# Second token parity wholly in Strassen groups, with the first parity's WO rows in place of its plain slots

## The chip, the cores and the metric

The kernel runs on one core of a Trainium2 chip. The metric is the device time of one execution in microseconds (us), as the median of several runs. A profiled execution gives the trace; its span goes from the first to the last instruction.

## The reference

For 2048 tokens of width D = 576 in float32 the reference normalises x and adds an attention and a feed-forward network that read the same normalised rows:

```python
x = A_x
xn = _layernorm(x, axis=-1)
return x + _A_ref(xn, A_wqkv, A_wo) + _B_ref(xn, B_w1, B_w2)
```

`_A_ref` projects xn by wqkv to q, k, v of 32 heads of 18, lets each token attend to 8 tokens (itself and the ones 2, 4, ... 14 before it), and multiplies the result by wo. `_B_ref` is `relu(xn @ w1) @ w2` with 4608 hidden columns. Since all distances in the attention are even, tokens of even and of odd position never meet.

## The kernel before

**Two parities.** The 1024 even tokens (ph 0) are worked off first, then the 1024 odd ones (ph 1). Each parity has four token blocks (tb) of 256 tokens. Every float32 operand is cut into a rounded high part and the remainder (`two`, L171: ACT writes the high part, VectorE or GpSimd the low one), and each product is made of three matmul terms: high x high, high x low, low x high. A matmul covers 64 of the 128 rows of the array; two of them, on the lower and the upper 64 rows, run at a time (`mm_rows`, `rows`), so work is counted in pairs. D is 4 x 128 + 64; the last 64 rows are the remainder.

**Plain slots.** A slot n is one block of 128 hidden columns f for one token block. For two slots `h_two` makes h with 14 + 13 pairs of 256 columns, `h_out` applies relu and cuts the result, and `o_two` makes the output matmuls of one slot, 6 pairs of 256 and 6 of 320 columns. The slots of a parity are numbered from `BASE[ph]`; each parity does its first 6 of 36 hidden blocks in 24 plain slots (`NOLD`). Lists by slot (`at`, `first`, `late`) place the other work between them: loads, cuts, the projection of the first head unit, the T sums, the preparation of the first Strassen pair.

**Strassen groups.** The remaining hidden blocks are taken two by two (a pair p). For a pair and 512 tokens a group g makes the 2 x 2 x 2 product of (2 x 128 hidden) x (2 x 256 of D) x (2 x 256 tokens) with 7 products in place of 8 (`PROD`, `M`), each 6 pairs, and adds the 64-row remainder (`R`, 6 pairs). It needs sums of W1's quarters, S1 to S4 (`sw_load`, `sw_mix`, `sw_prep`, staged in `ST`, put at the places in `MAT`), and sums of x^T's quarters, T1 to T4 (`ts_steps`, run in portions by `ts_run`). T1 to T4 of 512 tokens serve all groups of a parity. A group has eight steps; each step is 6 pairs of product and 6 pairs of output matmuls of the group before (`o_half`). Other work hangs on steps by `on(ph, g, i, "T" or "O", ...)`, and `ins` puts projections there. `prologue` is group 0, with the last plain output matmuls as filler; `tail_end` finishes a parity's last group. Before the change there are 15 pairs and 30 groups in each parity.

**Attention.** Heads are worked in four units u of 8 heads (`QKV_G` says with which group a unit's projection begins; unit 0 is projected among plain slots, at `UNIT0`). Its VectorE work waits in a queue, from which `run_bg` takes what fits. The result goes to DRAM (`od`), comes back transposed in four rows r of 256 tokens (`ot_in`, L697: one load of 512 KB and two of 64 KB), is cut by ACT and VectorE in two halves (`ot_split`, L708), and multiplied by wo (`wo_half`, four quarters a row, 54 pairs). `ot_plan` lists these steps with their conditions; `ot_go(ph)` does the next one that is due, `ot_go(ph, r)` does all that row r needs now. `evict` (L746) copies finished output tiles from PSUM on ACT and adds them to the output in DRAM with an accumulating DMA from GpSimd's queue; those of WO rows wait until the adds of all four token blocks have landed (`ADDED`).

**Between the parities.** x^T of the second parity is made early: normalised, turned, written to DRAM, and loaded back by `xt_in` (one load of 512 KB, two of 64 KB) into the buffer that the first parity's block leaves; `xt_parts` cuts it. In `seam` the first parity's last group ends with plain h matmuls of the second parity as filler, then WO row 0 follows; rows 1, 2 and 3 of the first parity stand at the second parity's slots 3 and 6. SyncE's queue (SP) issues all loads in the order of the program, each when its destination is free.

## Time and profile before

| | us |
|---|---|
| median of 3 runs (lowest, highest) | 1102.11 (1101.01, 1102.72) |
| profiled execution | 1100.51 |
| its span | 1098.7 |
| TensorE matmul busy | 1091.6 (99%) |
| VectorE busy | 837.8 (76%) |
| ScalarE busy | 573.3 (52%) |
| GpSimd busy | 269.7 (25%) |

PE is TensorE, PEld its weight loads, DVE VectorE, ACT ScalarE, POOL GpSimd, SP SyncE, and a q behind a name is that engine's queue. A row of a group of instructions names line, engine, operation, output<-input with their shapes and the count; behind the bar stand the busy time in us, the mean duration of one in ns, and the idle time of the engine before them with what ended it. A row of waits names who waited for whom, us in all, how often and the longest. In a timeline the first two numbers are start and length. A row of DMA issues gives the count, the KB of each, and the us from issue to landing. L numbers are lines of the kernel before.

### The profile page before, as it was taken

Reading aid. Unit: us, or ns where it says so; the run is one execution under the profiler, and the core shown is the slowest. Engines: PE = TensorE matmul, PEld = TensorE weight load, DVE = VectorE, ACT = ScalarE, POOL = GpSimd, SP = SyncE. Lnnn points to the kernel's source line nnn. Section 1 sums busy time; section 2 is a strip of 40 time slices with the busy share of each in tenths; the row PEclk is TensorE's granted clock in tenths of the full one; section 3 lists DMA queues with packets and bytes.
Section 4 is the critical chain, followed back from the end, with each engine's and each line's share of the span. In section 5 each row is a group of like instructions: output and inputs, shape, how many; then the busy total and the mean of one; then the engine's idle time right before and its main releaser. Section 6 shows DMA issues by size and latency. Waiting matters only on the chain.

```text
span 1098.7 us, 37877 instructions
## 1 busy us (share of the span) xinstructions
PE 1091.6 (99%) x16410; PEld 1085.1 (99%) x16410; DVE 837.8 (76%) x1379; ACT 573.3 (52%) x1353; POOL 269.7 (25%) x260
## 2 busy tenths in 40 slices
PE   9999999999999999999999999999999999999998
PEld 8999999999999999999999999999999999999998
DVE  7676888897997988994424549987989978998741
ACT  5433564564465356656634345635635644666551
POOL 2311421222222122322211022212212222223221
PEclk9999999999999999999999999999999999999999
DMA  7469995696598498889968159849947965988896
GB/s 227 149 158 225 176 200 98 146 214 116 104 231 145 72 224 160 156 151 255 271 94 188 24 119 188 149 77 198 183 88 162 207 113 109 220 148 168 163 226 150
DMA packets 136599, 177.26 MB, mean 161 GB/s; under 512 B 27873, under 2 KB 83937, under 8 KB 136401
## 3 DMA queue, kind: packets, MB, share of 16 engines
q0 software_dynamic: 37632, 81.40, 46.8%
q1 hardware_dynamic: 98080, 92.55, 29.4%
q8 instruction: 129, 2.11, 0.8%
q10 hardware_dynamic: 720, 0.89, 0.2%
q14 instruction: 38, 0.30, 0.1%
HBM read 74.07 MB, written 96.22 MB: 155 GB/s over the span
## 4 chain that ended last, share of the span: by engine, by line
PE 98%; DVE 1%; DMA 0%; ACT 0%; issue 0%; DVEq 0%; POOL 0%; ACTq 0%
PE po L163 34%; PE po L142 22%; PE ph L163 16%; PE pm L163 12%; PE pm L142 5%; PE ph L142 4%; PE ph L130 1%; PE po L130 1%; PE pm L354 0%; DMA att<-in_x 0%; DVE pr L575 0%; DMA words<-att 0%; PE pm L130 0%; DVE ar L176 0%; DVE att L419 0%
## 5 line engine op out<-in xcount | busy, mean ns | idle before, releaser
L163 PE MATMUL po<-ar 64*128 64x320 f32 (+1 forms) x5688 | 474.2, 289 | 0.1
L163 PEld LDWEIGHTS po<-ar 64*128 64x128 f32 x5688 | 416.3, 184 | 0.8 <-PE ph L163 0.4
L163 PE MATMUL ph<-xT,ar 64*128 64x256 f32 x2520 | 319.1, 274 | 1.0 <-DVE ar L807 1.0
L163 PEld LDWEIGHTS ph<-xT,ar 64*128 64x128 f32 x2520 | 287.7, 184 | 1.3 <-DVE ar L807 1.2
L762 POOL DMA_DIRECT2D out<-ev x126 | 151.4, 1201 | 554.4 <-ACT ev L756 391.1
L163 PE MATMUL pm<-xS,ar 64*128 64x256 f32 x2160 | 259.6, 274 | 0.0
L163 PEld LDWEIGHTS pm<-xS,ar 64*128 64x128 f32 x2160 | 238.4, 184 | 0.2
L756 ACT ACTIVATE ev<-po 128x640 f32<-128x640 f32 (+1 forms) x260 | 168.4, 652 | 132.7 <-PE po L163 75.3
L176 DVE TENSOR_TENSOR ar<-st,ar 128x256 fp32r<-128x256 f32 (+3 forms) x236 | 126.4, 556 | 58.7 <-ACT ar L172 56.5
L172 ACT ACTIVATE ar<-st 128x256 fp32r<-128x256 f32 (+3 forms) x304 | 146.6, 504 | 3.8 <-DMA st<-in_w 2.2
L142 PE MATMUL po<-wq,xT 64*128 64x432 f32 x1296 | 136.9, 354 | 0.0
L142 PEld LDWEIGHTS po<-wq,xT 64*128 64x128 f32 x1296 | 123.5, 184 | 1.9
L174 POOL TENSOR_TENSOR ar<-st,ar 128x256 fp32r<-128x256 f32 (+1 forms) x68 | 76.2, 1122 | 134.9 <-ACT ar L172 96.4
L163 PE MATMUL ph<-xS,ar 64*128 64x256 f32 x720 | 101.6, 274 | 0.0
L163 PEld LDWEIGHTS ph<-xS,ar 64*128 64x128 f32 x720 | 94.2, 184 | 0.1
L610 DVE TENSOR_TENSOR pr<-att 128x1152 f32<-128x1152 f32 x64 | 87.9, 1386 | 0.4
L575 DVE TENSOR_TENSOR pr<-att 128x1152 f32<-128x1152 f32 x64 | 86.3, 1359 | 0.1
L578 DVE TENSOR_REDUCE att<-pr 128x64 f32<-128x1152 f32 x64 | 85.8, 1345 | 0.0
L142 PE MATMUL po<-ar 64*128 64x256 f32 (+1 forms) x984 | 74.2, 289 | 0.0
L617 DVE TENSOR_TENSOR pr<-pr 128x1152 f32<-128x1152 f32 x64 | 68.9, 1076 | 1.4
L807 DVE SCALAR_TENSOR_TENSOR ar<-ph,ar 128x256 fp32r<-128x256 f32 x99 | 40.4, 420 | 37.7 <-ACT ar L803 37.5
L142 PEld LDWEIGHTS po<-ar 64*128 64x128 f32 x984 | 67.8, 184 | 0.3
(127 smaller groups left out, 1365.9 us busy)
## 6 DMA issues: line engine op xcount, KB each, us to landing
out<-ev POOLq DMA_DIRECT2D x126, 576.0 KB, 7.2
st<-in_w SPq DMA_DIRECT2D x72, 288.0 KB, 5.1
st<-in_w SPq DMA_DIRECT2D x63, 256.0 KB, 3.4
att<-att SPq DMA_DIRECT2D x16, 441.0 KB, 4.5
att<-in_wqkv SPq DMA_DIRECT2D x28, 216.0 KB, 6.2
od<-att SPq DMA_DIRECT2D x32, 160.0 KB, 6.1
att<-in_x SPq DMA_DIRECT2D x14, 288.0 KB, 4.0
st<-in_w SPq DMA_DIRECT2D x60, 64.0 KB, 6.1
```

Source lines behind the costliest of these rows:

```text
L142: ins = nc.tensor.matmul(o, l[z], r[z], start=start, stop=stop)
L163: b.ins = nc.tensor.matmul(b.ap, l[part], r[part], start=start, stop=stop, skip_group_check=skip)
L172: nc.scalar.activation(hi, src, AF.Copy)
L174: nc.gpsimd.tensor_tensor(lo, src, f32(hi), op=ALU.subtract)
L176: nc.vector.tensor_tensor(lo, src, f32(hi), op=ALU.subtract)
L575: nc.vector.tensor_tensor(pr[i], q, window(k, i), op=ALU.mult)
L578: nc.vector.tensor_reduce(lg[:, i], pr.pop(i).rearrange(heads, d=Dh), axis=AX.X, op=ALU.add)
L610: nc.vector.tensor_tensor(pr[i].rearrange(heads, d=Dh), e, window(v, i).rearrange(heads, d=Dh), op=ALU.mult)
L617: nc.vector.tensor_tensor(o, z[:, :, 0:n], z[:, :, n : 2 * n], op=ALU.add)
L756: nc.scalar.activation(acc[:, :, cols], z[:, :, 0 : cols.stop - cols.start], AF.Copy)
L762: ADDED[ph, tb] = nc.gpsimd.dma_start(rows_of(ph, tb), acc, accum_op=ALU.add)
L807: nc.vector.scalar_tensor_tensor(lo, src, 0.0, f32(hi), op0=ALU.max, op1=ALU.subtract)
```

## The change

The first parity stays as it was. The second parity has no plain slots any more: all its 36 hidden blocks are 18 pairs, 36 groups.

- `NP`, `NG` and the first hidden block `F0` now depend on the parity; `MAT` is one layout for both; a group number below 0 of the second parity means a group at the end of the first.
- The seam ends the first parity as the epilogue ends the second (`tail_pieces`), with output matmuls alone as filler. Then WO rows 0 and 1 follow back to back. The new `prologue` takes a function for its filler: for the second parity these are the quarters of WO rows 2 and 3, the last two of them in group 1.
- The T sums are made from the loaded x^T before it is cut (`apart`: four differences in place of four additions and four differences). Their steps and the cuts of x^T stand in a queue `side`, of which three are done after each quarter of a WO row.
- W1's first pair of the second parity is loaded, mixed and prepared in the last two groups of the first, two of its preparations in the seam.
- The projection of unit 0 moves into groups 3 and 4; units 1 to 3 come at groups 9, 15 and 21.
- The loads of WO rows 0 and 1 are allowed earlier (steps 4 and 5 of the last group), row 2's when the tail is done, row 3's when row 0 is done, into row 0's place.
- The room for two of the last evictions of the first parity is in pool xS in place of pr. The fourth mix of the first parity's pair 1 goes to GpSimd like its other three.

```diff
-UNIT0 = (10, 12)
-QKV_G = {0: -2, 1: 5, 2: 11, 3: 17}
+UNIT0 = 10
+QKV_G = ({1: 5, 2: 11, 3: 17}, {0: 3, 1: 9, 2: 15, 3: 21})
...
+    F0 = (NC0 * C, 0)
+    NP = [(NF - f) // 2 for f in F0]
+    NG = [2 * n for n in NP]
...
+        def apart(m, xt, k, b):
+            half = lambda z: z.rearrange("p (k c) -> p k c", k=2)
+            less_of = half(raw(b)) if isinstance(b, int) else f32(b[0][:, b[1] : b[1] + 2, :])
+            nc.vector.tensor_tensor(half(raw(m)), f32(xt[:, k : k + 2, :]), less_of, op=ALU.subtract)
+            dve(512)
+
+        if ph:
+            return [
+                (apart, 0, t2, 0, (t1, 0)), (apart, 1, t2, 2, (t2, 0)), (apart, 2, t2, 2, 0), (apart, 3, t1, 2, 2),
+                (cut, 0), (cut, 1), (cut, 2), (cut, 3),
+            ]
...
-        if r < 3:
-            z = ot_arena(ph)[:, r * OTW : (r + 1) * OTW]
+        if r < 3 or ph == 0:
+            k = r % 3
+            z = ot_arena(ph)[:, k * OTW : (k + 1) * OTW]
...
+        if g < 0:
+            ph, g = ph - 1, g + NG[ph - 1]
...
-        on(ph, NG - 1, 5, "O", hold.__setitem__, ("xs", ph), True)
-        on(ph, NG - 1, 1, "O", last_room, ph)
-        if ph == 0:
-            for i in range(2):
-                on(ph, NG - 1, 4 + i, "O", xt_in, 1, i)
-            on(ph, NG - 2, 4, "O", w1_load, 1, 0)
-            on(ph, NG - 1, 5, "O", w2_load, 1, 0)
-            on(ph, NG - 1, 5, "O", hold.__setitem__, ("go", 0), True)
-            on(ph, NG - 1, 5, "O", ot_go, 0)
...
+            on(ph, g, 4, "O", last_room, ph)
+            on(ph, g, 4, "O", xt_in, 1, 0)
+            on(ph, g, 4, "O", hold.__setitem__, ("go", 0), True)
+            on(ph, g, 4, "O", ot_go, 0)
+            on(ph, g, 5, "O", xt_in, 1, 1)
+            on(ph, g, 5, "O", hold.__setitem__, ("go", 1), True)
+            for i in (6, 7, 8):
+                on(ph, g, i, "O", ot_go, 0)
...
+    def sums(tp):
+        side.extend([(ts_run, 1, tp, 1)] * 4)
+        for i in range(4 * tp, 4 * tp + 4):
+            side.extend([(xt_parts, 1, i, 0), (xt_parts, 1, i, 1)])
+        side.extend([(low_twin, 1, 2 * tp)] + [(ts_run, 1, tp, 1)] * 4)
...
+        def more(k):
+            ot_go(0)
+            if k > 1:
+                xt_in(1, k)
+
+        tail_pieces(0, more, lambda: ot_go(0))
+        hold["go", 2] = True
+        for i in range(2):
+            w2_load(1, i)
+        sums(0)
+        side.extend([(sw_prep, 1, 0, "S3", "S4"), (sw_prep, 1, 0, "A22", "rem")])
+        for r in range(2):
+            for k in range(4):
+                ot_go(0, r) if k == 0 else ot_go(0)
+                wo_half(0, r, k % 2, k > 1)
+                aside(3)
+                if k == 2:
+                    ot_go(0, r + 1)
+            if r == 0:
+                hold["go", 3] = True
+        sums(1)
+
+    def wo_fill(n):
+        if n >= 8:
+            aside(len(side))
+            return
+        r, k = 2 + n // 4, n % 4
+        if k == 0:
+            ot_go(0, r)
+        wo_half(0, r, k % 2, k > 1)
+        ot_go(0)
+        aside(3)
+        if n == 1:
+            ot_go(0, 3)
...
+    prologue(0, old_fill)
+    for g in range(1, NG[0]):
+        group(0, g)
+    seam()
+    prologue(1, wo_fill)
+    for g in range(1, NG[1]):
+        group(1, g)
+    epilogue()
```

## The prediction

> **What bounds the kernel now.** I read the page first, then the waits of TensorE, then the stretch where the first parity ends (the seam): its engines by window, its chain, and the DMA queues.

> ```profile
> span 1098.7 us, 37877 instructions
> PE 1091.6 (99%) x16410; PEld 1085.1 (99%) x16410; DVE 837.8 (76%) x1379; ACT 573.3 (52%) x1353; POOL 269.7 (25%) x260
> ```
> ```profile
> PE po L119 <- POOL mhalf L114: 1.4, 1, 1.4
> PE ph L163 <- DVE ar L807: 1.0, 1, 1.0
> PE ph L130 <- ACT xT L359: 0.7, 1, 0.7
> PE pm L354 <- ACT att L338: 0.5, 1, 0.5
> ```
> TensorE waits 3.6 us in all, so the time is its list of matmuls, and a matmul less is time less as long as nothing new runs late. The prices, from the chain (half of a plain pair of slots, 28 matmuls; one whole WO row, 108), from the timeline (last two: 12 matmuls each) and from the windows (length, then busy time of PE, PEld, DVE, ACT, POOL, then the granted clock, DMA share, GB/s):

> ```profile
> 537.26 1.60 PE ph L142 x28
> 547.29 7.08 PE po L142 x108
> ```
> ```profile
> 1044.11 0.84 PE L163 MATMUL ph<-xT,ar 64*128 64x256 f32 x12
> 1044.79 0.84 PE L163 MATMUL po<-ar 64*128 64x256 f32 x12
> ```
> ```profile
> 515.57:530.01 14.44, 14.44 (x208) 13.77 (x209) 10.47 (x23) 11.95 (x29) 3.74 (x4) 1.00 1.10 277
> 1041.19:1052.87 11.68, 11.68 (x197) 11.68 (x194) 5.20 (x10) 7.76 (x20) 4.05 (x4) 1.00 1.03 255
> 1055.79:1066.45 10.66, 10.66 (x157) 10.31 (x154) 5.58 (x12) 6.87 (x14) 3.27 (x3) 1.00 1.04 207
> 1095.20:1098.70 3.50, 0.00 (x0) 0.00 (x0) 0.76 (x2) 0.00 (x0) 0.00 (x0) 0.90 0.46 156
> ```
> The 64-row matmuls run two at a time, so I count pairs. A plain pair of 256 columns costs 1.60/14 = 0.114 us, one in a Strassen group (1044.79 - 1044.11)/6 = 0.113 us. A whole group takes 11.68 us.

> **Term 1: the matmuls.** 24 plain slots of the second parity leave, 13.5 pairs each for h, 324 in all. In their place stand 6 groups: 7 products of 6 pairs and 6 pairs of remainder are 48, so 288. The output matmuls (12 pairs for a slot, 48 for a group), the four WO rows and the projections are as many as before. 36 pairs x 0.114 = **4.1 us less**; 72 matmuls fewer, 16338 on the page.

> **Term 2: the end of the first parity.** The seam took 14.44 us until its first WO row, with 27 pairs of plain h in it (27 x 0.114 = 3.08): 11.36 for the rest. The same tail at the end of the kernel, with only output matmuls as filler, took 10.66. The new seam has that second form and ACT no longer cuts x^T in it: **0.7 less**. Bounds: nothing, if ACT is as late as before, to 1.1, if no wait is left.

> **Term 3: the WO rows, now back to back.** Before, row 0 began at 530.01 and row 1 at 547.29, and rows 2 and 3 came after that. Now row 0 follows the tail (515.57 + 10.66 = 526.23), row 1 follows at 533.3, the first products at 540.39, and row 2 at 540.39 + 0.68 = 541.07. The row needs its 640 KB of attention output loaded and cut in two halves by ACT (L713) and DVE (L714). What speaks against that is DMA:

> ```profile
> DMA  9999999999999999999999999999999999999999
> q0 software_dynamic: 478, 1.06, 56.4%
> q1 hardware_dynamic: 1607, 1.69, 53.8%
> ```
> ```profile
> 516.20 1.59 SPq L706 DMA_DIRECT2D att<-od  x2
> 525.43 1.18 SPq L706 DMA_DIRECT2D att<-od  x2
> 534.66 1.64 SPq L706 DMA_DIRECT2D att<-od  x2
> ```
> ```profile
> att<-od SPq DMA_DIRECT2D x2, 64.0 KB, 9.0
> ```
> ```profile
> att<-od SPq DMA_DIRECT2D x2, 64.0 KB, 10.5
> ```
> ```profile
> att<-od SPq DMA_DIRECT2D x2, 64.0 KB, 8.6
> ```
> ```profile
> SPq L706 <- DMA xT<-words: 6.0, 3, 2.9
> ```
> From 525 to 535 us all 16 DMA engines are busy, and SP's queue (q1) moves 1.69 MB in 10 us, 0.169 MB/us; SP issues a load only when an older one has landed (the last row). The small parts of the loads of rows 0, 1, 2 were issued at 516.20, 525.43 and 534.66 and landed 9.0, 10.5 and 8.6 us later (the three rows, in that order; the issue of the second part adds up to 1.6). So row 2's data was whole at 543.3 to 544.9, say 544.1, while it was needed only after row 1, at 547.29 + 7.08 = 554.4.

> In the changed kernel row 2's load is again behind four x^T loads and two row loads, but two transfers are gone ahead of it: W1's first chunk (768 + 2x96 KB) becomes one pair's load (2x256 + 2x64 KB), 320 KB less, and of three loads of W2 (288 KB) two are left.

> ```profile
> st<-in_w SPq DMA_DIRECT2D x1, 768.0 KB, 10.1
> st<-in_w SPq DMA_DIRECT2D x2, 96.0 KB, 9.7
> ```
> ```profile
> st<-in_w SPq DMA_DIRECT2D x72, 288.0 KB, 5.1
> st<-in_w SPq DMA_DIRECT2D x63, 256.0 KB, 3.4
> st<-in_w SPq DMA_DIRECT2D x60, 64.0 KB, 6.1
> ```
> That is 608 KB or 0.62 MB, 3.7 us at SP's rate: row 2 whole at 540.4. The work of ACT and DVE on it:

> ```profile
> L713 ACT ACTIVATE att<-att 128x640 fp32r<-128x640 f32 x12 | 8.6, 735 | 0.9 <-DMA att<-od 0.9
> L432 ACT ACTIVATE xT<-xT 128x512 fp32r<-128x512 f32 x8 | 4.9, 623 | 0.0
> L438 ACT ACTIVATE xT<-xT 64x128 fp32r<-64x128 f32 x8 | 2.5, 311 | 0.2
> L756 ACT ACTIVATE ev<-po 128x640 f32<-128x640 f32 x131 | 92.5, 706 | 80.6 <-PE po L163 74.4 <-PE po L142 6.0
> L714 DVE TENSOR_TENSOR att<-att 128x512 fp32r<-128x512 f32 x12 | 8.3, 692 | 8.6 <-ACT att L713 8.3
> ```
> Two halves are 1.47 us on ACT, and DVE's low part comes 0.69 after the second, when TensorE has four pairs (0.45) of its own to do: 540.4 + 1.47 + 0.69 - 0.45 = 542.1. TensorE waits **1.0 us**. Bounds: nothing (whole by 539.4), and 4.7, if the place in the queue decides and not the bytes (544.1). I take the bytes, since the engines' line is full. Behind the waiting ACT stand row 1's second eviction, then the seed of product bank q and the copy of m5; TensorE reaches their buffers 2 us after row 2 begins, so the wait is paid once. Row 3's load waits on SP for row 0's end, and behind it stand only loads of the next pair.

> **Term 4: what ACT has left.** Beside rows 0 and 1 (14.16 us) ACT now does: four x^T parts (0.623 + 2 x 0.311 each, 4.98), four T cuts and two preparations of 512 columns (6 x 0.623, 3.74), a twin (64 rows by 256, between those two prices: 0.4), four evictions (2.82), and the four halves of rows 1 and 2 (2.94): 14.9 us by durations. Activations overlap; in

> ```profile
> 537.91 0.73 ACT L713 ACTIVATE att<-att 128x640 fp32r<-128x640 f32 x1
> 538.54 0.62 ACT L432 ACTIVATE xT<-xT 128x512 fp32r<-128x512 f32 x1
> ```
> the second starts 0.63 after a first of 0.73, which makes it 12.9 us. 1.3 us are to spare. Late seeds here, and the first projection weights of the parity (loaded half a group, 5.8 us, ahead of their cut, where

> ```profile
> att<-in_wqkv SPq DMA_DIRECT2D x28, 216.0 KB, 6.2
> ```
> says 6.2) I put at **0.5 us**, between 0 and 1.5.

> ```profile
> L973 DVE TENSOR_TENSOR st<-st 128x256 f32<-128x256 f32 x117 | 60.2, 516 | 5.0 <-DMA st<-in_w 3.6 <-POOL st L973 1.2
> L176 DVE TENSOR_TENSOR ar<-st,ar 128x512 fp32r<-128x512 f32 x92 | 60.9, 686 | 11.3 <-ACT ar L172 11.0
> L176 DVE TENSOR_TENSOR ar<-st,ar 128x256 fp32r<-128x256 f32 x96 | 39.4, 429 | 9.3 <-ACT ar L172 9.0
> ```
> At nothing I cost: DVE's T sums (8 operations of 512 columns fewer, 0.69 each as in L714, beside WO rows that need DVE for little else), the mixes and preparations of three more pairs (4 x 0.516 + 3 x 0.686 + 2 x 0.429 = 5.0 us of DVE for each; the 11.68 us group above holds 5.20 of DVE with its share of this and no wait of TensorE; uncovered, 5.0 us in two groups would show as waits at products), the fourth mix of one pair from DVE to POOL, and the room for two evictions in xS in place of pr (free three steps later).

> Sum: -4.1 - 0.7 + 1.0 + 0.5 = **-3.3 us**. The profiled execution took 1100.51 us (its span and 1.8 around it), so 1097.2 for it; it lies 1.6 under the median of the three runs, 1102.11, and from that I predict **1098.8**. A measurement of this kernel can tell about 0.2%, 2.2 us, from no change.

> **Rivals.** *Row 2 stays late* (chance 0.22): DMA is as full as before, and the two adds of row 0 to the output, which run once the last add has landed, now come into the time of row 2's load. For it: both queues hold over half of the engines. Against: 608 KB fewer. By the old landing: -4.8 + 4.7 + 0.5 = +0.4, 1102.5, no change.

> *The clock falls in that wait* (0.07). After the last matmul the row of 1095.20 shows a mean clock of 0.90 over 3.5 us: if that is half speed, it began 2.8 us after the last matmul. A wait of 2.8 to 4.7 at row 2 would then run the next 2.3 us (a row's quarter and six pairs) at half speed: -4.8 + 3.5 + 2.3 + 0.5 = +1.5, 1103.6. [...]

> *ACT stands before row 1* (0.13, the slower side). Row 1's first half is cut on ACT during row 0, ahead of evictions and x^T parts. If its data is late, ACT holds everything: row 2 can start at landing + 12.9 + 0.24. Row 1's load is now the fourth, with the bytes that row 0's had ahead of it before plus 32 KB: 516.20 + 9.0 + 1.0 + 0.2 = 526.4, free up to 527.9. But if it slips behind the third x^T load as before, it lands at 525.43 + 10.5 = 535.9: row 2 at 549.0, 8.0 us late, -4.8 + 8.0 + 0.5 = +3.7, 1105.8. It decides from a landing at 534.4 on. Against it: in the program its order to load comes two steps before that x^T load.

> **How the numbers follow.** My forecast has 0.58, and it holds while the waits come to less than 2.6 us of the 4.8 gained. So faster 0.58, same 0.22 + 0.07 = 0.29, slower 0.13. The forecast alone spans 1097.3 (no wait) to 1099.9; the range goes from 1096.8, with the scatter of the runs, up over the two middle cases to 1103.6.

> **What would show it.** 16338 matmuls or close to it; the tail in about 10.7 us; a wait of TensorE for ACT or DVE (L713, L714) at the third WO row, of about 1 us; groups of 11.68 us in the second parity from its first on; the granted clock at 1.00. I am wrong if TensorE's new waits add up to over 2.6 us, if they stand at a product (T sums or S matrices late) and not at a WO row, or if groups 3 to 9 of the second parity, with their projections, take more than 11.68 us and what their projections cost before.

## The result and the profile after

The changed kernel takes 1108.02 us (median of 6 runs, 1107.0 to 1109.93) where the kernel before takes 1102.05 in the same series (6 runs, 1101.01 to 1102.72): a ratio of 1.0057, 95% interval 1.0044 to 1.007. It is slower by 0.6%, clear of the scatter; 1098.8 was predicted. The profiled execution took 1107.0 us, 6.5 more than the one before. The mean granted clock was 0.995 or 0.997 in all six executions (0.997 in the profiled one), so the half clock shown below is not of this execution alone.

Lines of the changed kernel have other numbers: matmuls of Strassen groups and output L160 (before L163), of WO rows L139 (L142), cuts of attention rows L722 and L723 (L713, L714), the mixes L977 (L973). L1045 is the copy that seeds a product bank, L1054 an addition to a kept product. From the page of the changed kernel:

```profile
span 1105.2 us, 37855 instructions
PE 1092.0 (99%) x16338; PEld 1081.9 (98%) x16338; DVE 844.1 (76%) x1402; ACT 590.8 (53%) x1396; POOL 274.1 (25%) x267
```
The waits of TensorE in the changed kernel:
```profile
PE ph L160 <- ACT ph L1045: 6.1, 2, 4.8
...
PE po L139 <- DVE att L723: 0.6, 2, 0.4
PE po L139 <- ACT att L722: 0.5, 2, 0.3
```
The matmuls are 16338, as counted, and yet PE is as long busy as before. The first row is new: two waits at a product, one of 4.8 us. In windows of the changed kernel (length, busy time of PE, PEld, DVE, ACT, POOL, granted clock, DMA share, GB/s) stand the end of the first parity, rows 0 and 1, row 2's first quarter with the six pairs ahead of it, the last parity's tail, and from 1027.56 on the end of the long wait and what follows it:
```profile
516.69:527.36 10.67, 10.67 (x157) 10.33 (x155) 3.40 (x7) 5.56 (x12) 3.43 (x3) 1.00 1.11 267
527.36:542.21 14.85, 14.69 (x222) 14.49 (x220) 12.46 (x25) 12.05 (x27) 2.32 (x4) 1.00 1.07 263
542.21:546.33 4.12, 3.20 (x45) 2.61 (x43) 3.80 (x8) 2.22 (x4) 2.32 (x3) 1.00 1.05 200
1062.15:1072.81 10.66, 10.66 (x157) 10.31 (x155) 2.65 (x6) 4.73 (x10) 3.38 (x3) 1.00 0.75 110
1027.56:1030.97 3.41, 1.91 (x18) 1.91 (x20) 3.04 (x8) 2.95 (x8) 0.00 (x0) 0.50 1.10 324
1030.97:1034.38 3.41, 3.41 (x36) 3.41 (x36) 1.58 (x4) 1.63 (x6) 1.20 (x1) 0.50 1.12 296
1034.38:1038.00 3.62, 3.62 (x59) 3.62 (x59) 2.37 (x5) 2.95 (x7) 0.00 (x0) 1.00 0.92 182
```
TensorE idles for 4.8 us up to 1029.07 (its row is below) and then works at half clock until 1034.38. SP's queue in the changed kernel ahead of that, in its timeline, and its longest wait:
```profile
1008.12 1.81 SPq L647 DMA_DIRECT2D od<-att  x4
1016.97 0.34 SPq L264 DMA_DIRECT2D att<-wo  x1
...
1018.63 1.76 SPq L965 DMA_DIRECT2D st<-in_w  x2
1020.44 1.31 SPq L970 DMA_DIRECT2D st<-in_w  x2
```
```profile
SPq L264 <- DMA od<-att: 6.9, 1, 6.9
```
And DVE, ACT and TensorE in the timeline of the changed kernel:
```profile
1027.23 0.43 DVE L977 TENSOR_TENSOR st<-st 128x256 f32<-128x256 f32 x1 [7.37 <-DMA st<-in_w]
1027.57 0.41 DVE L1054 TENSOR_TENSOR m<-m,ph 128x256 f32<-128x256 f32 x1
...
1028.02 0.42 ACT L812 ACTIVATE ar<-m 128x256 fp32r<-128x256 f32 x1 [7.70 <-DVE m L1054]
...
1028.65 0.36 ACT L1045 ACTIVATE ph<-ph 128x256 f32<-128x256 f32 x1
...
1029.07 0.58 PE L160 MATMUL ph<-xS,ar 64*128 64x256 f32 x1 [4.81 <-ACT ph L1045]
```
This is one chain, read from the top. The attention's last stores (od) leave at 1008.12. The late WO load (L264 and its two small parts) writes over the buffer that they read, so it waits on SP until they have landed. Behind it stands the load of the last W1 pair (L965, L970). DVE reaches that pair's mix (L977) and stands, and behind the mix stands an addition that has nothing to do with it (L1054). ACT waits for the addition, and behind that stands the seed of TensorE's next product. Three queues in a row, each held by an instruction that isn't urgent.

In the kernel before the order at this place was the other one; its SP timeline:
```profile
1013.49 0.98 SPq L961 DMA_DIRECT2D st<-in_w  x2
...
1032.73 3.82 SPq L639 DMA_DIRECT2D od<-att  x4
1041.06 0.34 SPq L267 DMA_DIRECT2D att<-wo  x1
```
The last pair's load left 19 us ahead of the stores, and the WO load's wait held nothing up.

The smaller part of the first row of waits stands at the end of the first parity, where DVE stood at the mix of the second parity's first pair; in the timeline of the changed kernel:
```profile
509.48 0.38 PE L160 MATMUL ph<-xS,ar 64*128 64x256 f32 x1 [1.30 <-ACT ph L1045]
```

At row 2 two things are late by about the same, in the timeline of ACT in the changed kernel:
```profile
533.57 0.60 ACT L765 ACTIVATE ev<-po 128x512 f32<-128x512 f32 x1 [2.56 <-PE po L139]
...
542.63 1.36 ACT L722 ACTIVATE att<-att 128x640 fp32r<-128x640 f32 x2 [0.15 <-DMA att<-od]
```
ACT stands 2.56 us at the first eviction of row 0, which TensorE hasn't finished, and then works without a pause until 542.48; the load of row 2 lands 0.15 later.

**The sum.** The last tail of the first parity begins 1.12 us later (516.69 against 515.57), for the wait of 1.30 less 0.2 gained ahead of it. The tail takes 10.67 where the prediction's row gives 11.36 without the plain h: -0.69. The matmuls: -4.1. Rows 0 and 1 take 14.85 and not 14.16: +0.69. Row 2's stretch takes 4.12, its pairs 0.68 + 1.60: +1.84. The wait at the end is 4.81, and half clock from 1029.07 to 1034.38 loses half of 5.31, 2.66: +7.47. From the last tail to the end 43.05 against 42.91: +0.14. Together +6.5, and the spans differ by 6.5: nothing is left over, though the 4.1 is counted and not measured by itself.

### The profile page after: what moved, and what is told of

It is laid out like the page before. It is cut to its first block, busy times and chain, and to the rows that moved or that the text cites. A ratio compares the mean times of both kernels' runs of the same rounds, so it can differ in the third digit from the quotient of the medians.

```text
span 1105.2 us, 37855 instructions
## 1 busy us (share of the span) xinstructions
PE 1092.0 (99%) x16338; PEld 1081.9 (98%) x16338; DVE 844.1 (76%) x1402; ACT 590.8 (53%) x1396; POOL 274.1 (25%) x267
## 4 chain that ended last, share of the span: by engine, by line
PE 93%; DMA 4%; DVE 1%; SPq 1%; issue 1%; ACT 0%; POOL 0%; DVEq 0%; POOLq 0%; ACTq 0%
PE po L160 35%; PE po L139 19%; PE ph L160 18%; PE pm L160 14%; PE pm L139 2%; DMA st<-in_w 2%; PE ph L139 2%; PE ph L127 1%; DMA xT<-words 1%; PE po L127 1%; DMA att<-od 1%; SPq L398 1%; PE po L116 0%; PE pm L351 0%; DVE att L416 0%
## 5 line engine op out<-in xcount | busy, mean ns | idle before, releaser
L160 PE MATMUL po<-ar 64*128 64x256 f32 (+1 forms) x6240 | 498.4, 289 | 0.0
L160 PEld LDWEIGHTS po<-ar 64*128 64x128 f32 x6240 | 435.3, 184 | 0.4 <-PE ph L160 0.4
L160 PE MATMUL ph<-xT,ar 64*128 64x256 f32 x2772 | 348.8, 274 | 0.2 <-DVE ar L816 0.2
L160 PEld LDWEIGHTS ph<-xT,ar 64*128 64x128 f32 x2772 | 314.7, 185 | 0.7 <-DVE ar L816 0.4
L160 PE MATMUL pm<-xS,ar 64*128 64x256 f32 x2376 | 282.5, 274 | 0.0
L160 PEld LDWEIGHTS pm<-xS,ar 64*128 64x128 f32 x2376 | 259.7, 184 | 0.3
L765 ACT ACTIVATE ev<-po 128x512 f32<-128x512 f32 (+1 forms) x272 | 176.8, 652 | 115.5 <-PE po L160 83.1
L139 PE MATMUL po<-wq,xT 64*128 64x432 f32 x1512 | 156.4, 354 | 0.0
L139 PEld LDWEIGHTS po<-wq,xT 64*128 64x128 f32 x1512 | 138.4, 184 | 4.6
L160 PE MATMUL ph<-xS,ar 64*128 64x256 f32 x792 | 113.5, 277 | 6.1 <-ACT ph L1045 6.1
L160 PEld LDWEIGHTS ph<-xS,ar 64*128 64x128 f32 x792 | 104.9, 186 | 6.8 <-ACT ph L1045 6.6
L977 DVE TENSOR_TENSOR st<-st 128x256 f32<-128x256 f32 x128 | 62.6, 490 | 14.9 <-DMA st<-in_w 14.7
L541 ACT ACTIVATE att<-po 128x288 f32<-128x288 f32 (+1 forms) x88 | 28.7, 403 | 81.2 <-PE po L139 81.2
L160 PE MATMUL pm<-xT,ar 64*128 64x256 f32 x396 | 67.5, 276 | 0.1
## 6 DMA issues: line engine op xcount, KB each, us to landing
st<-in_w SPq DMA_DIRECT2D x72, 288.0 KB, 5.2
st<-in_w SPq DMA_DIRECT2D x69, 256.0 KB, 3.7
att<-in_wqkv SPq DMA_DIRECT2D x28, 216.0 KB, 6.8
att<-in_x SPq DMA_DIRECT2D x14, 288.0 KB, 4.1
```

Source lines behind the costliest of these rows:

```text
L139: ins = nc.tensor.matmul(o, l[z], r[z], start=start, stop=stop)
L160: b.ins = nc.tensor.matmul(b.ap, l[part], r[part], start=start, stop=stop, skip_group_check=skip)
L765: nc.scalar.activation(acc[:, :, cols], z[:, :, 0 : cols.stop - cols.start], AF.Copy)
L977: engine.tensor_tensor(stg(o), stg(a), stg(b), op=op)
```

## The experiments

The theory, called A throughout: the loss lies in the order on SP, where a load that waits for stores stands ahead of one that is urgent. Its rivals are that it lies in the amount of DMA traffic at that place, in DVE's mixes themselves, or in the seam. A ratio is the time of a version over that of the kernel before on the same chip, from all runs of both, with its 95% interval; the times beside it are medians, and their quotient is not exactly the ratio.

**1. The WO load behind the last W1 pair's load.**
```diff
-        f = (F0[ph] + 2 * p) * P
+        f, hold["sw", ph] = (F0[ph] + 2 * p) * P, p
...
-lambda: ph in ready and t["pe"] > ready[ph] + 4.0, ()))
+lambda: ph in ready and t["pe"] > ready[ph] + 4.0 and (ph == 0 or hold["sw", 1] == NP[1] - 1), ()))
```

> One edit to the changed kernel: the WO load of the second parity (lines 264 and 267, which stands on SyncE's queue until the stores of the last attention have landed, 6.9 us) may go only after W1's last pair has been loaded, so that the pair's four loads come first on the queue. Theory A (queue order): the 4.8 us wait of TensorE at 1024 us and the 5 us at half clock behind it (about 7.4 us in all) come from that order; both go, the time falls from 1108.0 to about 1100.6, and the loads are issued at 1011 to 1013 instead of 1018.6. Rival B (DMA is full there anyway): the loads still need 7 to 10 us to land, VectorE meets them late, TensorE keeps a wait of 1 to 3 us, time 1102 to 1105. Rival C (VectorE has too much to do with three more pairs): nothing changes, 1108.

Measured: 1098.9 us (12 runs, 1097.88 to 1101.79), ratio 0.9983, interval 0.9973 to 0.9992: faster than the kernel before. From its SP timeline and its waits of TensorE:
```profile
1006.91 1.82 SPq L647 DMA_DIRECT2D od<-att  x4
1011.01 2.14 SPq L965 DMA_DIRECT2D st<-in_w  x2
...
1016.02 0.35 SPq L264 DMA_DIRECT2D att<-wo  x1
```
```profile
PE po L139 <- ACT att L722: 0.9, 2, 0.6
PE ph L160 <- ACT ph L1045: 0.3, 1, 0.3
```
The same transfers in another order, the pair's load 7.6 us earlier, and by the two ratios (1.0057 and 0.9983) 0.74%, some 8 us, are gone. A holds; that the time is 1.7 below the 1100.6 that A gave fits the seam's wait, which this profile doesn't have either.

**2. The first mixes of the second parity's first pair later** (for the 1.30 at 509.48).
```diff
-for k, (d, i) in enumerate(((-2, 8), (-1, 1), (-1, 2)) if p > 1 or ph else ((-1, 3),) * 3):
+for k, (d, i) in enumerate(((-1, 4),) * 3 if ph and not p else ((-2, 8), (-1, 1), (-1, 2)) if p > 1 or ph else ((-1, 3),) * 3):
```

> One edit to the changed kernel: the first three mixes of the second parity's first W1 pair stand at step 4 of the first parity's last group, beside the fourth, in place of step 8 of the group before and steps 1 and 2. Theory A: VectorE no longer stands 3.9 us at a mix whose load has not landed (507.6 us), so the additions and relus behind it in its queue come in time, and TensorE's 1.3 us wait at 508 us goes: about 1106.8. Rival: the wait is of ACT's own making, or the four mixes in one place hold VectorE as long; then the wait stays or moves a step, 1108.

Measured: 1106.04 us (6 runs, 1102.67 to 1109.76), ratio 1.0047, interval 1.0029 to 1.0066. The wait near 509 is gone from its profile; the end's stays (2.2 us in that execution, the fastest of the six). So the seam's wait is a small part. It is in none of the three profiles with this edit (2, 4, 10) and in all but one of those without it (0.2 to 2.1 us; none in experiment 1).

**3. The two W2 loads behind row 2's load.**
```diff
         hold["go", 2] = True
-        for i in range(2):
-            w2_load(1, i)
         sums(0)
...
                 hold["go", 3] = True
+                for i in range(2):
+                    w2_load(1, i)
```

> One edit to the changed kernel: the two loads of W2 (288 KB each) for the second parity's first pair stand behind the load of WO row 2 on SyncE's queue instead of before it. Theory A (TensorE's 1.8 us at row 2 is its data landing late): 0.59 MB at 0.169 MB/us bring the data 3.5 us earlier, the wait goes to 0.3 or less, time about 1106.2. Rival (ACT's queue of cuts, T sums and evictions is what is late, not the data): ACT has no idle time before row 2's halves, the wait stays over 1 us, 1107.5 to 1108.

Measured: 1106.55 us (8 runs, 1100.22 to 1109.65), ratio 1.004, interval 1.002 to 1.006; its profile shows the end's wait again, 6.5 us. In it ACT went from a preparation of W1 straight to row 2's cut, without a wait for its data, and TensorE still waited at that row, 0.2 for ACT and 0.4 for DVE: there it is ACT's list of work, not the transfer. That holds for this execution; in others the load of row 2 lands later than ACT's list ends (experiments 4 and 10).

**4. All three together.**

> The three edits together. If the three waits are independent: 1108.0 - 7.4 - 1.3 - 1.8 = 1097.5, which is 4.5 us (0.4%) under the kernel before, and what is left over the sum of matmuls is the first two WO rows (14.85 us in place of 14.17). If the waits hide one another, the sum of the three single gains is larger than this one, and the time stays over 1099.

Measured: 1098.64 us (11 runs, 1097.07 to 1101.5), ratio 0.9978, interval 0.9969 to 0.9986. The first edit carries it; the others add nothing that can be told apart. Its profile shows something else, in windows at row 2:
```profile
541.50:544.92 3.42, 1.66 (x16) 1.07 (x15) 2.24 (x6) 1.95 (x3) 0.66 (x2) 0.98 1.05 279
544.92:548.33 3.41, 3.41 (x36) 3.41 (x34) 2.53 (x4) 0.12 (x1) 1.08 (x2) 0.52 1.11 287
```
No single wait there was over 1.11 us, but together they left TensorE idle for 1.76 of 3.42, and the clock fell for the next 3.4. ACT stood 1.01 us for row 2's load there, although the two W2 loads were behind it.

**5. The WO load on another queue**, at the same point of the program.
```diff
+        q = nc.gpsimd if ph and kt > 2 else nc.sync
         if kt < KT:
-            nc.sync.dma_start(lo, wo2[kt * UD : kt * UD + P, :])
+            q.dma_start(lo, wo2[kt * UD : kt * UD + P, :])
```
(and in the same way for its two small parts).

> The changed kernel, with one thing else: the second parity's late WO load (3 DMAs) is issued from POOL's queue in place of SP's, at the same point of the program. Theory A (SP's queue is in order, the WO load waits there 6.9 us for the attention output's stores, and the last W1 pair's load stands behind it): that load is issued about 7 us sooner, lands at about 1020, the wait of 4.8 us for the seed of product bank q near 1029 is gone and so is the half clock after it: span near 1098, median near 1101. Rival B (the bytes: stores, WO load and W1 load together are too much for the DMA engines at that place, whatever their order): the W1 pair still lands at 1025 or later, the wait stays at 3 us or more, and the median stays at 1106 to 1108. By A the price shows on POOL: its next add to the output is issued late by the 6.9 us or so, without a wait of TensorE.

Measured: 1109.12 us (4 runs, 1106.75 to 1109.23), ratio 1.0056, interval 1.0038 to 1.0073. No gain, against what A was said to give. From its SP timeline, its POOL timeline, and its waits of TensorE (its line numbers are one higher):
```profile
1013.98 2.20 SPq L966 DMA_DIRECT2D st<-in_w  x2
```
```profile
1019.83 0.61 POOL L265 DMA_DIRECT2D att<-wo  x1 [9.22 <-DMA st<-in_w]
...
1021.46 1.30 POOL L772 DMA_DIRECT2D out<-ev  x1
```
```profile
PE po L160 <- ACT ev L766: 5.4, 1, 5.4
```
The W1 pair's load is free (issued at 1013.98, 4.6 us earlier), and the wait for the seed's chain through DVE is gone. But POOL issued in order too: the WO load stands there for 9.2 us (the trace infers a load of weights as what ended that; the program's own condition is the landing of the stores), and behind it an add to the output, issued at 1021.46. Its eviction buffer comes free only when that add has landed, ACT stands at the next eviction, and TensorE waits for the PSUM bank (po) that this eviction is to empty. ACT stood 7.5 us for that landing. The wait went with the load to the queue that it was put in, at about the same price: 5.45 us and, at half clock until 1036.90, another 2.4. The mechanism of A is confirmed and its forecast for this run failed: I had left out who waits for the add.

**6. The same fault put into the first parity** (on top of experiment 1).
```diff
-t["pe"] > ready[ph] + 4.0
+t["pe"] > ready[ph] + 4.0 * ph
```

> The version that was faster (second parity's late WO load behind the last W1 pair's load), with the same fault put into the first parity: its late WO load is released as soon as the attention output's stores are issued, and so comes ahead of the load of the second parity's first W1 pair. Theory A: the wait appears there. SP stands at the WO load until the stores have landed, the W1 pair's load is issued 5 to 8 us later than the 497.7 of the changed kernel and lands after 511, DVE stands at the mixes, and TensorE waits 3 to 6 us for a seed (L1045) at 508 to 515, with the granted clock under 0.8 for some 5 us behind it where the wait is over 3: span 4 to 9 us above the 1097.0 of the faster version. Rival B (the place is harmless, since what made the load late at the end was the traffic there): no wait above 2 us, span 1097 to 1099.

Measured: 1102.84 us (10 runs, 1099.07 to 1107.42), ratio 1.0008, interval 0.999 to 1.0026: by the two ratios 0.25%, 2.8 us, above experiment 1, and the gain is gone. From its SP timeline, and TensorE's wait behind it in the timeline:
```profile
494.89 2.60 SPq L647 DMA_DIRECT2D od<-att  x4
499.63 0.34 SPq L264 DMA_DIRECT2D att<-wo  x1
...
501.33 1.04 SPq L965 DMA_DIRECT2D st<-in_w  x2
```
```profile
509.49 0.38 PE L160 MATMUL ph<-xS,ar 64*128 64x256 f32 x1 [2.12 <-ACT ph L1045]
```
In this execution the stores landed soon (the WO load left 4.7 us after their start, at the end of the changed kernel 8.9), and the wait was 2.1, less than the 3 to 6 expected, with a span of 1097.3; other executions of it reach 1107.4. This profile alone doesn't show the fault: with the loads in the other order the same place had waits of 1.34 (experiment 11) and 1.73 (7), and the pair's mix began at 507.65 here, in the changed kernel at 507.64. The median speaks for A, but its interval touches that of experiment 1. That the longer executions lose their time here is likely and not shown.

**7. Idle time made on purpose**: on top of experiment 1, ACT repeats the seed of bank q at four groups, 8, 10, 12 and 16 times more.
```diff
-        nc.scalar.activation(new_bank(ph, g, to).ap, B[ph, g, src].ap, AF.Copy)
+        z = new_bank(ph, g, to).ap
+        for _ in range(1 + EXTRA.get((ph, g, to), 0)):
+            nc.scalar.activation(z, B[ph, g, src].ap, AF.Copy)
```

> The faster version, with idle time of TensorE made on purpose: at four groups of the second parity ACT repeats the seed of product bank q 8, 10, 12 and 16 more times (0.37 us each, the same values again), so that TensorE must wait for it. Theory A (of the 7.4 us lost at the end of the changed kernel only 4.8 are the wait; the rest is the clock, which falls after about 3 us without matmuls and comes back some 5 us after): the waits under 2.5 us cost their own length and the clock stays at 1.00 in the windows behind them; those over 3 us show 0.50 behind them and cost 2 to 2.6 us more than their length. Rival (the clock is tied to the DMA traffic or to the place, not to the wait): no window behind a wait goes under 0.9, and each wait costs its length.

Measured: one run, 1116.67 us. The waits made so were 1.14, 2.02, 2.74 and 4.34 us; a fifth of 1.73, not made on purpose, stood in the seam. The fifth, the second and the third in its timeline, and windows of it behind the second, behind the third and behind the fourth:
```profile
509.72 0.38 PE L160 MATMUL ph<-xS,ar 64*128 64x256 f32 x1 [1.73 <-ACT ph L1047]
...
764.92 0.39 PE L160 MATMUL ph<-xS,ar 64*128 64x256 f32 x1 [2.02 <-ACT ph L1047]
...
975.82 0.38 PE L160 MATMUL ph<-xS,ar 64*128 64x256 f32 x1 [2.74 <-ACT ph L1047]
```
```profile
766.00:767.00 1.00, 1.00 (x17) 1.00 (x16) 1.00 (x2) 1.00 (x3) 0.00 (x0) 0.65 0.00 0
975.82:978.00 2.18, 2.18 (x38) 2.18 (x40) 1.18 (x2) 2.18 (x5) 0.00 (x0) 1.00 0.00 0
1003.92:1006.00 2.08, 2.08 (x18) 2.08 (x20) 1.08 (x2) 2.08 (x5) 0.00 (x0) 0.50 0.00 0
```
That the clock is a price of its own is confirmed (DMA was idle in the window at 766, where the clock fell, so it isn't the traffic). The threshold that I gave fell: 2.02 us were followed by half clock, which began at 766.3, 1.4 us after TensorE was at work again, and 2.74 us were not. The 1.73 in the seam were followed by it too, from 510.30 to 513.71.

**8. The quarters of WO rows 2 and 3 one place later** (on top of experiment 1).
```diff
-            wo_fill(i + 5)
+            wo_fill(i + 4)
+            if i == 3:
+                wo_fill(8)
...
-    prologue(1, wo_fill)
+    prologue(1, lambda k: wo_fill(k - 1) if k else ot_go(0, 2))
```

> The faster version, with each quarter of WO rows 2 and 3 put one place later among the first products of the second parity, so that row 2 begins after 12 pairs of products in place of 6, 0.68 us later; its cut on ACT stands where it stood. Theory A (row 2's rest of a wait, 0.9 on ACT and 0.6 on DVE, is the chain of ACT behind rows 0 and 1): up to 0.7 us of that goes, span 1096.3 to 1096.8 against 1097.0, median 0.3 to 0.7 lower, hardly to be told apart. Rival (the data of row 2 or x^T lands late and decides): the wait is moved and not less, or another appears at the seed of product bank r, whose cover is now a quarter in another place: the same time or slower by up to 1 us.

Measured: 1098.36 us (5 runs, 1098.07 to 1099.31), ratio 0.9968, interval 0.9955 to 0.998. The wait for L722 is gone from its profile (0.9 in experiment 1), that for DVE's low parts stays at 0.6; the interval overlaps that of experiment 1, so the gain itself isn't shown. Waits of 0.7 and 0.8 for seeds stand in its profile instead, at 414.5 and 509.2, both ahead of row 2 (the first is not near the end, where the expectation of experiment 10 below puts it).

**9. The projections two groups later**, with no other edit to the changed kernel.
```diff
-QKV_G = ({1: 5, 2: 11, 3: 17}, {0: 3, 1: 9, 2: 15, 3: 21})
+QKV_G = ({1: 5, 2: 11, 3: 17}, {0: 5, 1: 11, 2: 17, 3: 23})
```

> The changed kernel with one line of numbers else: the second parity's projections stand two groups later (groups 5, 11, 17, 23 of 36 in place of 3, 9, 15, 21), which puts the end of the attention as far ahead of the parity's end as it was before the change (13 groups). No condition is added. Theory A (the fault lies only in where the attention's end falls against the loads of W1 pairs: its stores, and the WO load that waits for them, came ahead of the last pair's load on SP): the stores come at about 1031, behind the last pair's load at 1011 to 1013, no wait for the seed of q at the end, span 1097 to 1099, median 1098.5 to 1100.5. Rival B (what cost the time is something that the change itself brings to the end of the kernel, and not this order): the wait stays, or 4 us and more are lost at another place, median 1104 to 1109.

Measured: 1099.38 us (10 runs, 1097.72 to 1102.01), ratio 0.9981, interval 0.997 to 0.9991. From its SP timeline:
```profile
1010.69 1.21 SPq L965 DMA_DIRECT2D st<-in_w  x2
...
1029.49 1.86 SPq L647 DMA_DIRECT2D od<-att  x4
1038.99 0.34 SPq L264 DMA_DIRECT2D att<-wo  x1
```
This is the order of the kernel before again, and its profile has no wait at the end. So the four group numbers of the projections alone turn the loss into a gain: the last projection stood 13 groups ahead of its parity's end before (17 of 30), 15 in the change (21 of 36), and 13 here.

**10 and 11. Edits together**: 1, 2 and 8; and 8 and 9.

> Three edits together: the second parity's late WO load behind the last W1 pair's load, each quarter of WO rows 2 and 3 one place later, and the first three mixes of the second parity's first pair one place later (group 29, step 4), so that they don't stand at DVE's head when their load is late. Against the version without the third edit (1098.36 us, waits of 0.8 for a seed near 509, and 0.7 near the end): theory A says that the 0.8 at 509 goes, span 1095.8 to 1096.4, median near 1097.8, 0.4% below before. Rival: the mixes' cover is gone, the preparations behind them are late and the wait comes back a step later: 1098.4 or slower.

> The two-groups-later projections and the quarters of WO rows 2 and 3 one place later, without the condition on the WO load. By theory A both faults are mended by placement alone: waits at the end and at row 2 under 1 us, span 1096 to 1097.5, median 1098 to 1099, as fast as the version with the condition. By rival B (see the run before) the end keeps 4 us or more of waits.

Measured: 1098.63 us (11 runs, 1097.18 to 1101.28), ratio 0.9975, interval 0.9967 to 0.9984; and 1098.64 us (10 runs, 1096.9 to 1100.25), ratio 0.9972, interval 0.9963 to 0.9981. Both forms of the mending give the same time, 0.25% to 0.3% below the kernel before. The 0.4% expected of the first wasn't reached. In its profile, of an execution of 1100.24 us, TensorE waited 1.0 for L722 again, since ACT stood for row 2's load; its ACT timeline:
```profile
542.14 1.36 ACT L722 ACTIVATE att<-att 128x640 fp32r<-128x640 f32 x2 [1.67 <-DMA att<-od]
```
Half clock followed from 544.47 to 547.88. In the seven profiles in which ACT stands for this load, its cut begins at 541.5 to 543.0, although row 0 begins between 525.3 and 527.4: what is saved ahead of the load is lost at it. All three profiles with edit 2 are among them, with stands of 1.0 us or more. Why the load doesn't land sooner isn't shown.

**12. Sixteen groups with repeats**, as in 7, 10 times each.

> The version with the WO load behind the last W1 pair's load, with ACT's repeats (10 each) at 16 groups of the second parity, so that TensorE waits about 2 us sixteen times, at different phases. In the run with four waits a fall of the clock followed a wait of 2.02 us and none followed one of 2.74; its fall and rise times (766.3, 769.6, 1001.9, 1008.6) lie whole multiples of 3.41 us apart. Theory A (the clock is decided once per window of 3.41 us that runs on by itself, by how much of it TensorE stood idle): some of the waits are followed by half clock and some are not; falls and rises lie on one grid of 3.41 us; a wait of 2 us that lies within one window is followed by a fall (1.7 us more), one that a window's edge cuts near its middle is not. Rival (the clock follows the length of the wait alone): waits of one length all do the same, whatever their place.

Measured: one run, 1168.78 us. TensorE waited 1.9 to 3.5 us at sixteen places. Two waits of one length in its timeline, and three windows (behind the first, behind the second, and behind a wait of 2.01 that ended at 982.76):
```profile
803.33 4.03 PE L139 MATMUL po<-wq,xT 64*128 64x432 f32 x24 [2.53 <-ACT ev L765]
...
906.12 1.04 PE L139 MATMUL po<-wq,xT 64*128 64x432 f32 x8 [2.53 <-ACT ev L765]
```
```profile
803.02:806.43 3.41, 3.10 (x18) 2.85 (x20) 2.14 (x3) 1.20 (x3) 1.20 (x1) 0.50 0.21 28
906.12:909.00 2.88, 2.88 (x30) 2.79 (x32) 1.91 (x3) 0.90 (x2) 1.20 (x1) 1.00 0.28 27
...
983.92:987.33 3.41, 3.41 (x38) 3.41 (x36) 3.13 (x7) 1.51 (x5) 1.21 (x1) 0.50 0.45 89
```
The first 2.53 brings half clock, the second doesn't; the rival is out. All 19 edges of the clock in this run between 600 and 1040 us, worked out from its granted clock in windows of 1 us, lie within 0.05 us of whole multiples of 3.413 from the first (983.92 - 803.02 = 180.90 = 53 x 3.413). On that grid the first wait had 2.2 us in one window, the second was cut in 1.81 and 0.72.

## Why the prediction was wrong

**What was right.** 36 pairs fewer: 16338 matmuls, as written. The tail in its second form: 10.67, written 10.66. A wait at row 2, for L722 and L723. With the end mended the time is 1098.4 to 1099.4 us in six versions, about the 1098.8 predicted for the change itself; that it comes so near is in part luck, as the other terms show.

**The step that failed** is "at nothing I cost ... the mixes and preparations of three more pairs". It priced DVE's time for a mix, 0.516 us, and asked what hides that. It did not ask when the load that feeds the mix is issued, on which queue, and what stands ahead of it there. The move of the projections to groups 9, 15 and 21 got no price at all, although it brings forward everything that hangs on the attention's end: the stores, the WO load that waits for them, and so the place of that load on SP against the loads of W1. That is +7.47, more than the whole +6.5, shown from both sides: undone by order (experiment 1), undone by placement (9), and moved to another engine with the load (5). Put in elsewhere (6) it is likely and not shown. The text even named the sign by which it would be wrong, waits at a product, and then searched for them among T sums and S matrices at the start of the parity only.

**The other terms.** Row 2 was written at 1.0, for its data alone, and measured 1.84. The step that failed there is "1.3 us are to spare" on ACT: 12.9 us of work were set against 14.16, but ACT stands 2.56 of them at row 0's first eviction, and its list ended 15.1 us after row 0's start (542.48 against 527.36). Where the data is in time, that list alone costs 1.5 to 1.6 (experiments 3, 6 and 9); where the load lands later still, and half clock follows, the stretch has lost 3.5 to 4.1 (2, 4 and 5). The start of row 0 was not priced and costs 0.69: ACT begins its cut at 525.93, behind an eviction of the tail, and DVE's second low part (L723) ends at 528.43, when TensorE has been in row 0 for 1.1 us. The 0.5 for late seeds became the 1.30 at 509.48, where DVE stood at the first pair's mix; from the mix on it is the chain of the end, smaller, and in versions that have the same program there it is anything from nothing to 1.73 (experiments 1, 8, 11, 7: none, 0.78, 1.34, 1.73). One term put at nothing was a gain, "the fourth mix of one pair from DVE to POOL". In the kernel before, DVE stood at that mix and TensorE then waited 0.98 for L807, up to 124.80; DVE's row there:
```profile
119.68 0.42 DVE L973 TENSOR_TENSOR st<-st 128x256 f32<-128x256 f32 x1 [1.25 <-POOL st L973]
```
In the changed kernel 0.22 is left of the wait. It had been 0.34 behind the kernel before at 116.3 and is 0.29 ahead at 124.51, so 0.6 are gained; in experiment 9, with no wait there, 1.2. It is the fault of the end in small, and the change took it away without the prediction's knowing.

In the version of experiment 9 the terms give -0.36 (row 0 at 525.88, less the tail's 10.67, against 515.57) - 0.69 - 4.1 + 0.71 (row 0 to the first product at 540.75) + 1.54 (from there to the next product at 544.57) = -2.9, and its span, 1095.9, is 2.8 below that of before. The -0.36 hides a wait of 0.68 in the seam and the 1.2 just named. So what the prediction left out came out nearly even, the mix against row 0 and the rest of row 2, and the nearness to -3.3 is luck to that extent.

**The rivals.** *Row 2 stays late* came true by 1.84 us, not 4.7. *ACT stands before row 1* did not occur. *The clock falls in that wait* had the right mechanism: in the changed kernel's profile the clock fell at the end and not at row 2, in those of experiments 2, 4, 5 and 10 at row 2 too. Its condition, a wait of 2.8 us or more, was wrong (4, 7, 12). That its price, 2.3 us, lies near the 2.66 at the end is chance: it was an estimate of how much work would run at half clock, and in the runs half clock lasted one step of 3.41 us (4, 10) or two, 6.82 (the changed kernel).

## What to carry to other kernels

When a change moves a block of work against another, list every DMA that hangs on either, in the order in which its queue issues them, and look for one that waits for a transfer and has something urgent behind it: here a load that stood 6.9 us on SP led to a loss of 7.47. Do the same on DVE and ACT: here a mix that was not urgent held DVE for 7.37 us, and ACT stood 7.70 for the addition behind it, ahead of the seed. Moving the waiting load to a queue that had something urgent of its own gained nothing (1109.12 us, experiment 5); placing it behind the urgent one gave 1098.9 (experiment 1), moving what it waits for 1099.38 (9). And time saved ahead of a load that landed no sooner was lost again at that load: where ACT stood for it, row 2's cut began at 541.5 to 543.0, wherever between 525.3 and 527.4 row 0 had begun.

## What was not expected of the hardware

**Times scattered more in the version with the fault.** The kernel before lies between 1100.30 and 1104.22 in 25 runs beside experiments 1 to 4; a version with the fault between 1100.22 and 1109.65 in 8 (experiment 3). The profiles show the same wait at 2.2 us in experiment 2 and 6.5 in experiment 3; behind the second the clock fell, behind the first not. There is one profile of each version, so that the landing of transfers makes the whole scatter is likely and not shown.
